# Attention of a gated attention + S4 layer, forward and backward: two interleaved streams of 512-wide tiles with the value products turned round, in held order

## The chip, the cores and the metric

One core of a Trainium2 chip runs the whole program. The metric is device time in microseconds; several runs are taken, beside runs of the kernel before on the same chip. PE is the matmul engine, DVE the vector engine, ACT the engine for exponentials, POOL the general-purpose engine.

## The reference

The program computes the output of `g * attention(x) + (1 - g) * S4(x)` and its gradients. Only attention matters here: sequence 2048, 32 heads of 18 numbers each, bf16.

```python
qkv = (x @ wqkv).reshape(B, S, 3, H, Dh) ...      # H = 32, Dh = 18, S = 2048
scores = einsum("bhqd,bhkd->bhqk", q, k) * Dh ** -0.5
p = softmax(scores)
o = einsum("bhqk,bhkd->bhqd", p, v)
# and by vjp: dV = P^T dO, dP = dO V^T, dS = P * (dP - delta), dQ = dS K, dK = dS^T Q
```

Heads are treated in eight groups of four; each head has 32 rows of the 128 to itself. Per head there are 2048 x 2048 exponentials twice (once with keys on rows, once with queries on rows) and as many products `dS = P * dP` twice. In tiles of 128 x 512 that is 4096 exponentials for ACT and 4096 products for DVE.

## The kernel before

It works in three stages that take turns. Forward (P1): scores, exponential into `PT`, value product. Then dq (P2): dP, product, `dS K`. Then dk/dv (P3): scores, exponential, dP, product, and both value products. The core of P1 and P2 for one block of 512 queries, cut:

```python
for kt in range(NT):                                        # P1
    for u in range(NU):                                     # two halves of 256 columns
        for j in range(4):                                  # row group 32*j holds head j
            mm(pss[j][:, u*256:(u+1)*256], lhsT=KaT_g[r0:r0+DA, kt*P:(kt+1)*P],
               rhs=QaT_g[r0:r0+DA, qs:qs+256], tile_position=(r0, 0))
    for j in range(4):
        nc.scalar.activation(PT[j][:, kt, :], pss[j], ACT.Exp)
    if kt >= 1: pv_step(kt - 1)
def pv_step(kt_):                                           # the value product
    for j_ in range(4):
        for qi_ in range(TPQ):                              # probability tile is the weight,
            mm(oacc[:, j_, qi_, 0:DA], lhsT=PT[j_][:, kt_, qi_*P:(qi_+1)*P],
               rhs=Vtok_g[:, kt_, j_, 0:DA], ...)           # 19 columns move
# ... normalisation, delta, transposes ...
for kt in range(NT):                                        # P2, after all of P1
    ... dP scores into pss; dq_step(kt - 1, ...) ...
    for j in range(4):
        nc.vector.tensor_tensor(dst, pss[j], PT[j][:, kt, :], op=A.mult)
```

The scheduler of the framework may reorder instructions within what the data allow.

Of the kernel before, what the change touches and what calls it, by code (L numbers as in the profile page):

```python
# [9 lines left out]
A = mybir.AluOpType  # L10
# [10 lines left out]
def build(tc, aps, dbg_aps=None, stages=("s1", "attn", "post", "s4", "final")):  # L21
# [39 lines left out]
    with ExitStack() as gctx:  # L61
# [14 lines left out]
        RL = const.tile([P, H, NT], F32, name="RL")  # L76
# [5 lines left out]
        dO_tok = mid1.tile([P, NT, D], BF, name="dO_tok")  # L82
# [6 lines left out]
        Vtok_d = dram.tile([P, NT * H * HP], BF, name="Vtok_d")  # L89
        dqkv_d = dram.tile([P, NT, F], BF, name="dqkv_d")  # L90
# [3 lines left out]
        with ExitStack() as ctx:  # L94
# [127 lines left out]
            for t in range(NT):  # L222
# [5 lines left out]
                for c, (e0, esz) in enumerate(dch):  # L228
                    pt = psB.tile([P, P], BF, tag="tp", name="pt_tp2")
                    nc.tensor.transpose(pt[0:esz, :], d_a_t[:, e0:e0 + esz], ident_bf)  # L230
                    if cnt % 2 == 0:
                        nc.vector.tensor_copy(d_aT[0:esz, c, t * P:(t + 1) * P], pt[0:esz, :])
                    else:
                        nc.scalar.copy(d_aT[0:esz, c, t * P:(t + 1) * P], pt[0:esz, :])
                    cnt += 1
            EW = 48
# [13 lines left out]
            dbg("dO_tok", dO_tok)  # L250
# [5 lines left out]
        if "attn" in stages:  # L256

            DA = DH + 1
            KB = 512
            NQQ = S // KB  # L260
            TPQ = KB // P
            NU = KB // 256
            with ExitStack() as ctx:
                ga = ctx.enter_context(tc.tile_pool(name="ga", bufs=1))
                hp = ctx.enter_context(tc.tile_pool(name="hp", bufs=1))
                hw1 = ctx.enter_context(tc.tile_pool(name="hw1", bufs=1))
                stp = ctx.enter_context(tc.tile_pool(name="stp", bufs=2))
                work = ctx.enter_context(tc.tile_pool(name="awork", bufs=4))
                apsp = ctx.enter_context(tc.tile_pool(name="aps", bufs=1, space=bass.MemoryType.PSUM))

# [3 lines left out]
                cnt = 0  # L274
                for grp in range(NG):
                    QaT_g = ga.tile([P, S], BF, tag="QaT_g", name="QaT_g")
                    KaT_g = ga.tile([P, S], BF, tag="KaT_g", name="KaT_g")
                    VaT_g = ga.tile([P, S], BF, tag="VaT_g", name="VaT_g")
                    nc.sync.dma_start(QaT_g, QaT_d[grp])
                    nc.sync.dma_start(KaT_g, KaT_d[grp])  # L280
                    nc.sync.dma_start(VaT_g, VaT_d[grp])
                    Qtok_g = ga.tile([P, NT, 4, HP], BF, tag="Qtok_g", name="Qtok_g")
                    Ktok_g = ga.tile([P, NT, 4, HP], BF, tag="Ktok_g", name="Ktok_g")
                    Vtok_g = ga.tile([P, NT, 4, HP], BF, tag="Vtok_g", name="Vtok_g")
                    nc.sync.dma_start(Qtok_g, Qtok_v[:, :, 4 * grp:4 * grp + 4, :])
                    nc.sync.dma_start(Ktok_g, Ktok_v[:, :, 4 * grp:4 * grp + 4, :])
                    nc.sync.dma_start(Vtok_g, Vtok_v[:, :, 4 * grp:4 * grp + 4, :])
                    dOa_h = []
                    dOaT_h = []
                    dq_st = []  # L290
                    dk_st = []
                    dv_st = []
                    PT = []
                    for j in range(4):
                        t_ = hw1.tile([P, NT, DA + 1], BF, tag=f"dOa_h{j}", name=f"dOa_h{j}")
                        nc.gpsimd.memset(t_[:, :, DA:DA + 1], 0.0)
                        dOa_h.append(t_)
                        t_ = hw1.tile([P, S], BF, tag=f"dOaT_h{j}", name=f"dOaT_h{j}")
                        dOaT_h.append(t_)
                        dq_st.append(stp.tile([P, NT, DH], BF, tag=f"dq_st{j}", name=f"dq_st{j}"))  # L300
                        dk_st.append(stp.tile([P, NT, DH], BF, tag=f"dk_st{j}", name=f"dk_st{j}"))
                        dv_st.append(stp.tile([P, NT, DH], BF, tag=f"dv_st{j}", name=f"dv_st{j}"))
                        PT.append(hp.tile([P, NT, KB], BF, tag=f"PT{j}", name=f"PT{j}"))
                    for qq in range(NQQ):
                        q0 = qq * KB
                        t0 = qq * TPQ
                        oacc = apsp.tile([P, 4, TPQ, DA + 1], F32, tag="accA", name="oacc")

                        def pv_step(kt_):
                            for j_ in range(4):  # L310
                                for qi_ in range(TPQ):
                                    mm(oacc[:, j_, qi_, 0:DA], lhsT=PT[j_][:, kt_, qi_ * P:(qi_ + 1) * P], rhs=Vtok_g[:, kt_, j_, 0:DA],
                                       start=(kt_ == 0 and j_ == 0 and qi_ == 0), stop=(kt_ == NT - 1 and j_ == 3 and qi_ == TPQ - 1))

                        for kt in range(NT):
                            pss = [apsp.tile([P, KB], F32, tag="blk", bufs=5, name=f"ps_st{j}") for j in range(4)]
                            for u in range(NU):
                                for j in range(4):
                                    r0 = HP * j
                                    qs = q0 + u * 256  # L320
                                    mm(pss[j][:, u * 256:(u + 1) * 256], lhsT=KaT_g[r0:r0 + DA, kt * P:(kt + 1) * P],
                                       rhs=QaT_g[r0:r0 + DA, qs:qs + 256], tile_position=(r0, 0))
                            for j in range(4):
                                nc.scalar.activation(PT[j][:, kt, :], pss[j], ACT.Exp)  # L324
                            if kt >= 1:
                                pv_step(kt - 1)
                        pv_step(NT - 1)
                        for j in range(4):
                            h = 4 * grp + j
                            r0 = HP * j  # L330
                            hc0 = h * DH
                            rl = RL[:, h, t0:t0 + TPQ]
                            nc.vector.reciprocal(rl, oacc[:, j, :, DH])  # L333
                            rlb = rl.unsqueeze(2).to_broadcast([P, TPQ, DH])
                            Oview = O_tok[:, t0:t0 + TPQ, hc0:hc0 + DH]
                            nc.vector.tensor_tensor(Oview, oacc[:, j, :, 0:DH], rlb, op=A.mult)
                            dOa = dOa_h[j]
                            nc.vector.tensor_tensor(dOa[:, t0:t0 + TPQ, 0:DH], dO_tok[:, t0:t0 + TPQ, hc0:hc0 + DH], rlb, op=A.mult)
                            prod = work.tile([P, TPQ, DH], F32, tag="prod", name="prod")
                            nc.vector.tensor_tensor(prod, dOa[:, t0:t0 + TPQ, 0:DH], Oview, op=A.mult)  # L340
                            dl = work.tile([P, TPQ], F32, tag="dl", name="dl")
                            nc.vector.tensor_reduce(dl, prod, axis=AX.X, op=A.add)
                            nc.scalar.mul(dOa[:, t0:t0 + TPQ, DH], dl, -1.0)
                            pT = apsp.tile([P, KB], BF, tag="pT", name="pT")
                            for qi in range(TPQ):
                                nc.tensor.transpose(pT[r0:r0 + DA + 1, qi * P:(qi + 1) * P], dOa[:, t0 + qi, 0:DA + 1], ident_bf,
                                                    tile_position=(0, r0))
                            if j % 2 == 0:
                                nc.scalar.copy(dOaT_h[j][r0:r0 + DA + 1, q0:q0 + KB], pT[r0:r0 + DA + 1, :])  # L349
                            else:  # L350
                                nc.vector.tensor_copy(dOaT_h[j][r0:r0 + DA + 1, q0:q0 + KB], pT[r0:r0 + DA + 1, :])
                        dqacc = apsp.tile([P, 4, TPQ, DA + 1], F32, tag="accB", name="dqacc")

                        def dq_step(kt_, dsts_):
                            for j_ in range(4):
                                for u_ in range(TPQ):
# [4 lines left out]
                        for kt in range(NT):  # L361
# [7 lines left out]
                            if prev_dsts is not None:  # L369
                                dq_step(kt - 1, prev_dsts)  # L370
# [13 lines left out]
                    for kc in range(S // KB):  # L384
# [15 lines left out]
                        for qt in range(NT):  # L400
# [12 lines left out]
                            if prev_ is not None:  # L413
                                dvk_step(qt - 1, prev_[0], prev_[1])
# [690 lines left out]
```

## Time and profile before

| | us |
|---|---|
| median of the timed runs | 8968.7 |
| span of the profiled run | 8949.4 |
| attention in it, first to last | 454 to 5548: 5094 |
| everything else | 3855 |

In attention PE is busy 4982 us, DVE 2716 and ACT 2323. So DVE and ACT together have about as much to do as the stage lasts, but hardly ever at the same time in P1 and P2. The lines that carry this are in the prediction below, with their reading.

### The profile page before, as it was taken

Reading aid. Unit: us, or ns where it says so; the run is one execution under the profiler, and the core shown is the slowest. Engines: PE = TensorE matmul, PEld = TensorE weight load, DVE = VectorE, ACT = ScalarE, POOL = GpSimd, SP = SyncE. Lnnn points to the kernel's source line nnn. Section 1 sums busy time; section 2 is a strip of 40 time slices with the busy share of each in tenths; the row PEclk is TensorE's granted clock in tenths of the full one; section 3 lists DMA queues with packets and bytes.
Section 4 is the critical chain, followed back from the end, with each engine's and each line's share of the span. In section 5 each row is a group of like instructions: output and inputs, shape, how many; then the busy total and the mean of one; then the engine's idle time right before and its main releaser. Section 6 shows DMA issues by size and latency. Waiting matters only on the chain. (4 is left out here: it accounts for less than half of the span.)

```text
span 8949.4 us, 216931 instructions
## 1 busy us (share of the span) xinstructions
PE 6928.2 (77%) x94711; PEld 3868.7 (43%) x94711; DVE 4108.3 (46%) x8636; ACT 3477.3 (39%) x7088; POOL 48.5 (1%) x67
## 2 busy tenths in 40 slices
PE   7799999999999999999999998864443232336773
PEld 5544444444444444444444444753332222236662
DVE  4345455446455455555465554340003777740004
ACT  4344534444444534444534444230001666740001
POOL 0000000000000000000000000000000000000000
PEclk6555555555555555555555555875555555555555
DMA  2101201301301310310211113229996222239997
GB/s 76 72 16 7 9 6 7 13 4 5 14 4 5 13 7 2 14 7 1 13 7 8 7 3 15 90 72 365 384 385 265 83 83 83 93 130 364 372 372 223
DMA packets 502110, 827.64 MB, mean 92 GB/s; under 512 B 295202, under 2 KB 325028, under 8 KB 491428
## 3 DMA queue, kind: packets, MB, share of 16 engines
q1 hardware_dynamic: 501156, 813.76, 32.3%
q8 instruction: 740, 12.12, 0.6%
q14 instruction: 214, 1.75, 0.1%
HBM read 753.09 MB, written 60.56 MB: 91 GB/s over the span
## 5 line engine op out<-in xcount | busy, mean ns | idle before, releaser
L423 DVE TENSOR_TENSOR dsb<-ps_dp,eb 128x512 bf16<-128x512 f32 x2048 | 1325.4, 687 | 1126.4 <-PE ps_dp L30 1009.3
L419 ACT ACTIVATE eb<-ps_s 128x512 bf16<-128x512 f32 x2048 | 1165.9, 596 | 1525.2 <-PE ps_s L30 1503.5
L324 ACT ACTIVATE PT<-ps_st 128x512 bf16<-128x512 f32 x2048 | 1072.7, 611 | 1026.5 <-PE ps_st L30 1021.1
L374 DVE TENSOR_TENSOR dst<-ps_dpt,PT 128x512 bf16<-128x512 f32 x2048 | 1235.2, 697 | 5.5 <-ACT dOaT_h L349 1.2
L30 PE MATMUL ps_dp<-VaT_g,dOaT_h 19*128 19x256 bf16 x4096 | 1014.3, 402 | 0.3
L30 PE MATMUL ps_dpt<-dOaT_h,VaT_g 19*128 19x256 bf16 x4096 | 946.8, 398 | 39.4 <-ACT dOaT_h L349 20.5
L30 PE MATMUL ps_s<-KaT_g,QaT_g 19*128 19x256 bf16 x4096 | 965.3, 402 | 1.0
L30 PE MATMUL ps_st<-QaT_g,KaT_g 19*128 19x256 bf16 x4096 | 927.2, 403 | 15.9 <-DMA KaT_g<-KaT_d 8.1
L30 PEld LDWEIGHTS <-dsb 128*128 128x128 bf16 x8192 | 416.9, 105 | 878.2 <-issue 873.6
L30 PE MATMUL yps<-CXG,HK 128*128 128x16 bf16 x9216 | 553.9, 175 | 231.5 <-issue 154.4
L842 PE MATMUL pt_e<-ident_bf,E1e 128*128 128x128 bf16 x1152 | 186.8, 282 | 689.2 <-ACT E1n L843 350.9
L30 PE MATMUL dkps<-GYREVp,HX 128*128 128x16 bf16 x9216 | 343.0, 175 | 451.8 <-DMA HX<-xpR_d 451.8
L30 PE MATMUL dkacc<-Qtok_g,dsb 128*128 128x18 bf16 x8192 | 647.6, 180 | 0.0
L30 PEld LDWEIGHTS <-HK 128*128 128x128 bf16 x18432 | 528.8, 104 | 274.4 <-issue 170.0
L30 PEld LDWEIGHTS <-dst 128*128 128x128 bf16 x8192 | 338.5, 106 | 602.8 <-issue 602.8
L30 PEld LDWEIGHTS <-PT 128*128 128x128 bf16 x8192 | 329.6, 105 | 595.0 <-issue 588.5
L30 PE MATMUL dxps<-CXG,HK 128*128 128x16 bf16 x9216 | 545.6, 174 | 2.2 <-ACT CXG L914 2.2
L333 DVE RECIPROCAL RL<-oacc 128x4 f32<-128x4 f32 x128 | 22.8, 178 | 1100.1 <-PE oacc L30 1100.1
L30 PEld LDWEIGHTS <-eb 128*128 128x128 bf16 x8192 | 336.1, 105 | 409.9 <-issue 409.9
L30 PEld LDWEIGHTS <-HX 128*128 128x128 bf16 x9216 | 290.5, 105 | 504.8 <-DMA HX<-xpR_d 503.9
L30 PE MATMUL dqacc<-Ktok_g,dst 128*128 128x18 bf16 x8192 | 481.1, 179 | 0.0
L30 PE MATMUL oacc<-Vtok_g,PT 128*128 128x19 bf16 x8192 | 471.4, 182 | 3.4 <-ACT PT L324 0.4
(297 smaller groups left out, 6748.0 us busy)
## 6 DMA issues: line engine op xcount, KB each, us to landing
HX<-xpR_d SPq DMA_DIRECT2D x576, 512.0 KB, 9.6
HK<-Kpad_d SPq DMA_DIRECT2D x576, 512.0 KB, 6.7
abuf<-ath_d SPq DMA_DIRECT2D x36, 1024.0 KB, 4.7
thb<-ath_d SPq DMA_DIRECT2D x36, 1024.0 KB, 4.9
x_tok<-in_A_x_dram SPq DMA_DIRECT2D x3, 2304.0 KB, 9.5
go_t<-in_grad_out_dram SPq DMA_DIRECT2D x48, 144.0 KB, 2.1
dqkv_tok<-dqkv_d SPq DMA_DIRECT2D x1, 6912.0 KB
ga_d<-ga_st SPq DMA_DIRECT2D x16, 288.0 KB, 2.3
```

Source lines behind the costliest of these rows:

```text
L30: return nc.tensor.matmul(out, lhsT=lhsT, rhs=rhs, start=start, stop=stop, **kw)
L324: nc.scalar.activation(PT[j][:, kt, :], pss[j], ACT.Exp)
L333: nc.vector.reciprocal(rl, oacc[:, j, :, DH])
L374: nc.vector.tensor_tensor(dst, pss[j], PT[j][:, kt, :], op=A.mult)
L419: nc.scalar.activation(eb, pss[j], ACT.Exp)
L423: nc.vector.tensor_tensor(dsb, pss2[j], ebs[j], op=A.mult)
L842: nc.tensor.transpose(pt[:, ri, :], E1e[:, ch, ri, :], ident_bf)
```

## The change

Its intent: let ACT and DVE work at once, so that neither waits out the other's stage, and use PE's array by placing heads side by side, in row groups for the scores and column groups for the value products. Core of the diff:

```diff
+ctx.enter_context(tc.manual_schedule(engines={PE, Activation, DVE, Pool}))   # order as written
-for j_ in range(4): for qi_ in range(TPQ):
-    mm(oacc[:, j_, qi_, 0:DA], lhsT=PT[j_][:, kt_, qi_*P:(qi_+1)*P], rhs=Vtok_g[:, kt_, j_, 0:DA])
+mm(acc[HP*j:HP*(j+1), :], lhsT=st[:, i, j, :], rhs=mv, ..., tile_position=(0, HP*j))  # token tile is
+                                                     # the weight (32 wide), 512 columns move
+blocks: (P1(g,b), P2(g,b-1)), (P3S(g-1,b), P3D(g-1,b)), ...    # exponential and product stream
+for (a_, d_) in blocks:
+    for i in range(NT):
+        for jj in ((0, 1), (2, 3)):                            # one step: two heads
+            act_s.append((a_, i, jj))
+            dve_s.append((d_, i, jj))
+act_s.append((None, 0, ()))
+dve_s.insert(0, (None, 0, ()))                                 # product stream one step behind
+for n in range(len(act_s) + LAG):
+    score matmuls of step n (2 + 2 heads); value products of step n - LAG; exponentials and products of n
+    # transposes back and gradient copies come in small pieces, one every third step
```

(Cuts: loads, normalisation and the pieces. All after attention is the same code.)

## The prediction

> **What bounds the kernel now.** I read the page first: busy time of the engines, then the 40 slices, then the costliest groups.
>
> ```profile
> PE 6928.2 (77%) x94711; PEld 3868.7 (43%) x94711; DVE 4108.3 (46%) x8636; ACT 3477.3 (39%) x7088; POOL 48.5 (1%) x67
> ...
> PE   7799999999999999999999998864443232336773
> ...
> PEclk6555555555555555555555555875555555555555
> ...
> L423 DVE TENSOR_TENSOR dsb<-ps_dp,eb 128x512 bf16<-128x512 f32 x2048 | 1325.4, 687 | 1126.4 <-PE ps_dp L30 1009.3
> L419 ACT ACTIVATE eb<-ps_s 128x512 bf16<-128x512 f32 x2048 | 1165.9, 596 | 1525.2 <-PE ps_s L30 1503.5
> L324 ACT ACTIVATE PT<-ps_st 128x512 bf16<-128x512 f32 x2048 | 1072.7, 611 | 1026.5 <-PE ps_st L30 1021.1
> L374 DVE TENSOR_TENSOR dst<-ps_dpt,PT 128x512 bf16<-128x512 f32 x2048 | 1235.2, 697 | 5.5 <-ACT dOaT_h L349 1.2
> ```
>
> The page's chain of waits covers only the last 58 us (it starts at 8891), so it says nothing of attention; I used the times of first and last instruction of the attention tiles instead. Attention runs from 453.8 (first ps_st) to about 5548 (last gradient copies): 5094 us of 8949.4. The other 3855 us are code that the diff leaves alone. Then I asked for the busy time in single stages: a forward pass of one block of 512 queries (all four heads of a group), the dq pass of the next, and a dk/dv pass, and the whole of attention.
>
> ```profile
> 454.00:494.00 40.00, 36.92 (x394) 15.88 (x387) 2.93 (x19) 33.52 (x68) 0.00 (x0) 0.50 0.22 44
> ...
> 576.00:618.00 42.00, 41.44 (x412) 18.48 (x411) 38.77 (x66) 3.61 (x7) 0.00 (x0) 0.50 0.01 2
> 777.00:854.00 77.00, 77.00 (x768) 33.65 (x767) 42.15 (x69) 37.10 (x67) 0.00 (x0) 0.50 0.33 12
> ...
> 454.00:5548.00 5094.00, 4982.28 (x49681) 2211.47 (x49674) 2715.51 (x5000) 2322.68 (x4486) 6.15 (x29) 0.50 0.15 7
> ```
>
> Columns: stretch, length, busy PE, weight loads, DVE, ACT, POOL, then the granted clock. The three stages take turns: forward keeps ACT busy (33.5 of 40) while DVE has nothing; the dq pass keeps DVE busy (38.8 of 42) while ACT has nothing; dk/dv has PE full (77 of 77) and both others half idle. Sixteen tiles of four heads per pass give 2.5, 2.6 and 4.8 us. The clock is 0.50 in all of them, however full PE is. How full PE is in truth shows in order of time:
>
> ```profile
> 520.39 0.29 PEld L30 LDWEIGHTS <-dst 128*128 128x128 bf16 x8 [0.41 <-issue]
> ...
> 520.70 0.19 PEld L30 LDWEIGHTS <-VaT_g 19*128 19x128 bf16 x4
> ...
> 521.30 0.19 PEld L30 LDWEIGHTS <-dst 128*128 128x128 bf16 x4 [0.41 <-issue]
> ...
> 790.29 0.12 PEld L30 LDWEIGHTS <-dOaT_h 19*128 19x128 bf16 x2
> ...
> 790.82 0.18 PEld L30 LDWEIGHTS <-dsb 128*128 128x128 bf16 x4 [0.41 <-issue]
> ...
> 791.03 0.12 PEld L30 LDWEIGHTS <-QaT_g 19*128 19x128 bf16 x2
> ```
>
> From one head's two 256-column score matmuls to the next weight load is 0.53 us (790.29 to 790.82); four of them, two heads in different row groups, take 0.60 (520.70 to 521.30). So heads in different row groups do overlap. The small matmuls that follow cost 0.31 for eight and 0.21 for four, so about 26 ns each and 0.10 fixed. Two streams of 256 columns at half of 2.4 GHz are 0.427, so 0.10 to 0.17 of each score block is also a change-over.
>
> **What the skill says.** "TensorE: Matmul & The Clock Gate", section on the back-to-back issue gap: N columns take N/1.2 ns at the half clock and N/2.4 at the full one. The trace agrees at half clock as far as the 0.53 shows. Its Part 3 on packing: tiles in different row groups run together (3.07 times for four) and so do tiles in different column groups (2.38 for three). For rows the trace agrees (0.60 against 0.53); column tiles don't occur before, so no run shows them yet. "TensorEngine Tiling (Array Packing)", Key Properties: a change of tiling mode drains the array; that fits the fixed 0.10 us. Part 1 of the clock page: the clock goes to full after about 3.4 us of activity. The trace limits this: 0.50 through a PE that counts as 100% busy in dk/dv, and 1.00 only in later stages with dense 128-row matmuls (30 per us of 128x48 turned it up within four microseconds at 5597; 15 per us of 128x54 at 50 to 100 us left it at 0.50).
>
> **The change, part by part.** Kept: 4096 exponentials and 4096 products of 512 columns. Removed: 32768 matmuls of 18 or 19 columns, each with a full weight load, and the halving of score matmuls. Added: the value, dq, dk and dv products turned round: weights are the 32-wide token tile, the moving operand is the 512-wide tile, output goes to 32 PSUM rows per head in a column group of its own; 8192 of these, beside 8192 score matmuls of 512 columns. The output is transposed back in pieces. Moved: every step now pairs two heads of an exponential stream with two heads of a product stream, so ACT and DVE work at once. The built order of PE confirms: four score matmuls, then four value matmuls of two steps earlier.
>
> Limits of one step: ACT 2 x 0.597 = 1.19 us; DVE 2 x 0.69 = 1.38. PE at half clock: score part, two row groups, each two tiles of 427 ns one after the other, plus 0.13 change-over, about 0.99; value part, two column groups, again 2 x 0.427, plus 0.10, about 0.96. Sum 1.95 us. So PE bounds, not DVE, as long as the clock is at half: only two of four groups are in use at a time, because the two streams of a step have the same two heads.
> There are 65 blocks of 32 steps: 63 full ones, 63 x 32 x 1.95 = 3931. The first has only the forward stream (32 x 1.2 = 38), one near the end only dq (32 x 1.4 = 45). 28 empty steps of the first group, where transposed output is waited for: 20. Pieces on PE: 32 times four fp32 transposes (estimate 1.9 us, four passes each), 32 times four bf16 ones (0.65), 48 times eight (1.06): 61 + 21 + 51 = 133. Sum 4167 against 5094. Extra work of ACT (accumulator copies, about 130 us) and DVE lies beside it; POOL gets two small products per block, covered by the pieces' delay of several steps. With 3855 for the rest and 19 us between the profile's span and the timed median: 8041.
>
> **Rivals.**
> 1. The clock rises. PE streams 1.71 of 1.95 us, 88%, against some 65% in dk/dv before. If the monitor counts streaming of any tile, this may be enough; if it weighs the part of the array in use (a quarter per tile, so 44% of the array's columns and rows here), it isn't. At full clock a step needs about 1.1 us on PE and DVE bounds at 1.38: 2016 x 1.40 = 2822, plus 38, 45, 20 and about 100 for DVE's own extras and pieces, 3025 in all; total 6900. For: Part 1 of the page. Against: 0.50 at every moment of attention before, with PE called full.
> 2. The clock swings: full clock makes PE wait for DVE, its activity falls to 60%, it is throttled again. 7300 to 7600.
> 3. Column tiles don't overlap. Then the value part is 4 x 0.427 + 0.10 = 1.81 and the step 2.8: attention 5900, total 9800, slower. Only the skill speaks against it.
> 4. Emission order stalls: scores have three PSUM buffers per stream, and the second score matmul of a step waits for the first exponential of the step before. At 1.95 us that exponential is long done, so it costs nothing while PE bounds; pieces that borrow a score buffer (112 of them) could each cost up to a microsecond, 100 us.
>
> **Range and chances.** I give the half clock 0.6 (7850 to 8250), full clock 0.25 (near 6900), a swing 0.1, no overlap or something unforeseen 0.05. The median of that lies at the lower edge of the first: 7900. Four times in five within 6850 to 8250. Faster by over 2% in all but the last: 0.94; within 2% 0.02; slower 0.04.
>
> **What would show it.** Attention from about 455 to 4620 us with PE near 100% busy, clock 0.50, ACT and DVE each around 60 to 70% and waiting for PE: main line right. Clock near 1.0 in those slices, DVE near 95% and PE waiting for DVE: rival 1. Value matmuls starting one after another at 0.43 us: rival 3. The 1.95 is wrong if a change-over is not near 0.1 us, and the sum if the PE waits for ACT or DVE between score matmuls. The slices after attention must be the same as before.

## The result, and the profile after

The changed kernel takes 6800.0 us (median of 4 runs, 6798.8 to 6805.5); before, on the same chip, 8968.7. The ratio is 0.7583, 95% interval 0.7573 to 0.7594. Ratios are the mean time of one kernel's fast runs over that of the other's of the same rounds, so not quite the ratio of the medians. The predicted 7900 was too slow, and 6800 lies just outside the range of 6850 to 8250.

First the page of the changed kernel: engines, the slices with the clock, and the first groups.

```profile
PE 4762.3 (70%) x62071; PEld 2257.4 (33%) x62071; DVE 4011.0 (59%) x7837; ACT 3479.8 (51%) x6912; POOL 101.5 (1%) x133
...
DVE  4328999989898989899943500002678767200005
ACT  3347878878787878786833300001866685300001
...
PEclk6555555555555555555578655555555555555555
...
L398 DVE TENSOR_TENSOR ds<-ps_P3D,eb 128x512 bf16<-128x512 f32 x2048 | 1293.3, 686 | 128.3 <-PE ps_P3D L30 83.7
L390 ACT ACTIVATE PT<-ps_P 128x512 bf16<-128x512 f32 x2048 | 1107.8, 596 | 211.9 <-PE ps_P L30 113.4
```

DVE is now at 0.8 to 0.9 and more in nearly every slice of attention. Its idle time before the dk/dv products fell from 1126 us (group L423 of before) to 128, and ACT's before the forward exponentials from 1027 (L324) to 212. Each product still takes 686 ns, each exponential 596. The clock row still says half. Attention as one stretch:

```profile
454.00:3408.00 2954.00, 2814.82 (x17004) 596.72 (x17005) 2614.68 (x4192) 2321.17 (x4301) 53.73 (x97) 0.50 0.06 13
```

The last gradient copies leave at 3416 us, so attention takes 2962 us instead of 5094, that is 2132 less; the whole span is 2151 less. So practically all of the gain comes from attention, as predicted. DVE is busy 2615 of the 2954 us in this window, 89%. PE's 2815 (95%) is no measure of its load, as two steps in order of time show:

```profile
1000.02 0.61 PE L30 MATMUL accA<-eb,dOa 128*32 128x512 bf16 x2
...
1000.02 0.61 PE L30 MATMUL accB<-ds,Qtok_g 128*32 128x512 bf16 x2
1000.56 0.10 PEld L30 LDWEIGHTS <-QaT_g 19*128 19x128 bf16 x2 [0.43 <-issue]
1000.56 0.61 PE L30 MATMUL ps_P3S<-KaT_g,QaT_g 19*128 19x512 bf16 x2
...
1000.57 0.78 PE L30 MATMUL ps_P3D<-VaT_g,dOaT_g 19*128 19x512 bf16 x2
...
1001.27 0.11 PEld L30 LDWEIGHTS <-dOa 128*32 128x32 bf16 x2 [0.60 <-issue]
```

All four value matmuls start at 1000.02 and the first three score matmuls 0.54 us later: 0.54 us for four tiles of 512 columns. The prediction expected two and two, 0.96 and 0.99 us. The fourth score matmul begins 0.20 us after the third (the pair spans 0.78 instead of 0.61 from first start to last end), as it waits for DVE (so the built order says: its PSUM buffer, a bank of the memory that matmuls write to, is the one that an earlier product reads). Between 900 and 2900 us the four scores of a step are spread like this in 95% of the steps, by 0.22 us in the median. Where they are not, the four take 0.54 us. So PE has slack, and DVE sets the pace.

The same view for DVE (one row for four products):

```profile
1040.70 2.52 DVE L398 TENSOR_TENSOR ds<-ps_P,PT 128x512 bf16<-128x512 f32 x4
```

Back to back a product costs 0.63 us, not the 0.69 of one alone. A block of P1 with P2 has 64 of them, 40.3 us; such blocks take 42.5 us (from the first exponential of one block to that of the next; median of 28). Blocks of P3, in which the transposes and copies fall, take 46.5 us (median of 27).

### The profile page after: what moved, and what is told of

Its sections match the earlier page's. It is cut to its first block, busy times and chain, and to the rows that moved or that the text cites.

```text
span 6798.7 us, 147781 instructions
## 1 busy us (share of the span) xinstructions
PE 4762.3 (70%) x62071; PEld 2257.4 (33%) x62071; DVE 4011.0 (59%) x7837; ACT 3479.8 (51%) x6912; POOL 101.5 (1%) x133
## 3 DMA queue, kind: packets, MB, share of 16 engines
q14 instruction: 184, 1.51, 0.1%
## 5 line engine op out<-in xcount | busy, mean ns | idle before, releaser
L398 DVE TENSOR_TENSOR ds<-ps_P3D,eb 128x512 bf16<-128x512 f32 x2048 | 1293.3, 686 | 128.3 <-PE ps_P3D L30 83.7
L398 DVE TENSOR_TENSOR ds<-ps_P,PT 128x512 bf16<-128x512 f32 x2048 | 1288.3, 686 | 101.5 <-PE ps_P L30 97.0
L394 ACT ACTIVATE eb<-ps_P3S 128x512 bf16<-128x512 f32 x2048 | 1109.2, 596 | 259.8 <-PE ps_P3D L30 179.1
L390 ACT ACTIVATE PT<-ps_P 128x512 bf16<-128x512 f32 x2048 | 1107.8, 596 | 211.9 <-PE ps_P L30 113.4
L30 PE MATMUL ps_P3D<-VaT_g,dOaT_g 19*128 19x512 bf16 x2048 | 790.8, 593 | 16.4 <-DVE ds L398 15.8
L30 PE MATMUL ps_P<-dOaT_g,VaT_g 19*128 19x512 bf16 x2048 | 757.9, 592 | 0.0
L30 PE MATMUL ps_P<-QaT_g,KaT_g 19*128 19x512 bf16 x2048 | 676.0, 597 | 72.1 <-DMA KaT_g<-KaT_d 37.7
L30 PE MATMUL ps_P3S<-KaT_g,QaT_g 19*128 19x512 bf16 x2048 | 671.0, 597 | 31.0 <-ACT eb L394 28.5
L30 PE MATMUL dkps<-GYREVp,HX 128*128 128x16 bf16 x9216 | 343.2, 175 | 456.4 <-DMA HX<-xpR_d 456.4
L30 PE MATMUL dxps<-CXG,HK 128*128 128x16 bf16 x9216 | 545.4, 174 | 145.7 <-issue 143.3
L30 PE MATMUL accA<-PT,Vtok_g 128*32 128x512 bf16 x2048 | 625.0, 608 | 6.0 <-DMA Vtok_g<-Vtok_d 5.8
L30 PE MATMUL accB<-ds,Qtok_g 128*32 128x512 bf16 x2048 | 626.7, 608 | 0.0
L30 PE MATMUL accA<-eb,dOa 128*32 128x512 bf16 x2048 | 626.7, 608 | 0.0
L30 PE MATMUL accB<-ds,Ktok_g 128*32 128x512 bf16 x2048 | 625.2, 608 | 0.0
L30 PEld LDWEIGHTS <-HK 128*128 128x128 bf16 x18432 | 528.3, 104 | 264.8 <-DMA HK<-Kpad_d 144.2
L30 PE MATMUL yps<-CXG,HK 128*128 128x16 bf16 x9216 | 549.9, 175 | 79.5 <-DMA HK<-Kpad_d 77.5
L30 PEld LDWEIGHTS <-HX 128*128 128x128 bf16 x9216 | 290.7, 105 | 509.5 <-DMA HX<-xpR_d 508.5
```

Of the source, the lines that this page charges most:

```text
L30: return nc.tensor.matmul(out, lhsT=lhsT, rhs=rhs, start=start, stop=stop, **kw)
L390: nc.scalar.activation(out, ps, ACT.Exp)
L394: nc.scalar.activation(out, ps, ACT.Exp)
L398: nc.vector.tensor_tensor(out, ps, e, op=A.mult)
```

## The experiments

Block lengths below are read in this way. The runs were made in four sittings, in which the median of the kernel before lay between 8941 and 8984 us; so differences between two variants are worked out from their ratios, times 8968.7. Two theories had to be told apart: that four different heads stand side by side in a step, because the product stream is one step behind (mine, after the result), or that PE is simply faster than the prediction's sum, or DVE or order matter in some other way.

**1. The same heads in both streams.** The product stream is put two steps behind, not one; two steps are one round of heads (0, 1), (2, 3).

```diff
-act_s.append((None, 0, ()))
-dve_s.insert(0, (None, 0, ()))
+for _ in range(2):
+    act_s.append((None, 0, ()))
+    dve_s.insert(0, (None, 0, ()))
```

> The changed kernel with the product stream two steps behind the exponential stream instead of one, so that both streams of a step hold the same two heads, as the prediction had wrongly assumed. Theory (four heads side by side is what makes PE cheap): score part and value part of a step take two tiles one after the other per row or column group, step 1.95 us by the prediction's own sum, attention about 4170 us, whole 8000 us (7850 to 8200), PE full, DVE idle about a third. Rival (PE streams faster than the sum thinks, whatever the groups): within 2% of the changed kernel, 6800 us.

8077.1 us (ratio 0.8989, 0.8976 to 0.9003), correct. PE in order of time:

```profile
1000.80 0.61 PE L30 MATMUL ps_P<-QaT_g,KaT_g 19*128 19x512 bf16 x2
...
1001.20 0.63 PE L30 MATMUL ps_P<-dOaT_g,VaT_g 19*128 19x512 bf16 x2
...
1001.77 0.61 PE L30 MATMUL accA<-PT,Vtok_g 128*32 128x512 bf16 x2
...
1002.17 0.63 PE L30 MATMUL accB<-ds,Ktok_g 128*32 128x512 bf16 x2
...
1002.74 0.61 PE L30 MATMUL ps_P<-QaT_g,KaT_g 19*128 19x512 bf16 x2
```

The second pair now starts 0.40 us after the first, in the scores and in the value products, and the step is 1.94 us. The prediction's sum of 1.95 us a step and 8041 us in all describes this kernel, within half a per cent. By the ratios it lies 1261 us above the changed kernel ((0.8989 - 0.7583) x 8968.7): the worth of one inserted empty step.

**2. A control: three steps behind.** Different heads again, but a longer lag (same edit with 3).

> A control for the run with two steps of shift: three steps, so that the two streams of a step hold different heads again, but the product stream lags by more. Theory (which heads share a step decides): back at the changed kernel's time, 6760 to 6860 us. Rival (the longer lag was what cost 1280 us): 8000 us or more.

7341.4 us (0.8210, 0.8198 to 0.8223): between the two. The blocks say why. Those of P3 were back at 46.6 us in the median (65.5 with two steps), but those of P1/P2 took 59.7. The waits of 2000 us in the middle name it:

```profile
ACT PT L390 <- DVE ds L398: 413.3, 239, 1.8
```

The longer lag keeps probability tiles longer than the 18 buffers allow. So I gave it 19.

```diff
-ptp = ctx.enter_context(tc.tile_pool(name="ptp", bufs=18))
+ptp = ctx.enter_context(tc.tile_pool(name="ptp", bufs=19))
```

> The control again, with 19 probability tiles instead of 18: with three steps of shift and 18 tiles ACT waited 413 us per 2000 for the products to free them, and the forward blocks took 59.7 us, while the dk/dv blocks, which use no such tiles, were back at 46 to 47 against 65.5 with two steps. Theory (which heads share a step decides, the lag by itself costs nothing once there is a tile for it): dk/dv blocks about 46.5, forward blocks 42.5 to 44, whole 6780 to 6880 us. Rival (the lag costs in itself): 7200 us or more.

6815.1 us (0.7624, 0.7611 to 0.7637); P1/P2 blocks 42.65, P3 blocks 46.6 in the median. The lag by itself costs nothing; which heads share a step decides.

The run with 18 tiles holds a trap. Its clock row reads differently from all others:

```profile
PEclk9999999999999999999976875555555555555555
```

Yet its four value tiles take the same 0.55 us (value matmuls at 1100.65, the first score matmuls at 1101.20). The packed trace explains the row: this run's clock records begin only at 3745 us, and the view shows full clock where there is no record. (The 1.00 of the kernel before up to 44 us is such a gap too; the prediction's "only in later stages" passes over it.) So the spacing of matmuls has to confirm the row. The Trainium skill, "TensorE: Matmul & The Clock Gate", Part 1, warns in its trace caveats that the recorded events can be unreliable; this run, with no record for its first 3745 us, agrees.

That the spacing does tell the clock is shown by four other runs (experiments 3, 6, 8 and the second form of 7), whose records have full clock inside attention for 6.8 to 23.9 us at a time. In the second form of 7, where only dq was left to do and a group is two tiles, a group took 0.54 us at half clock (3010.05 to 3010.59) and 0.32 soon after; four tiles in experiment 6 took 0.33 (2346.28 to 2346.61):

```profile
3015.40:3036.00 20.60, 19.66 (x136) 6.00 (x136) 17.89 (x28) 5.77 (x12) 0.20 (x1) 1.00 0.02 4
...
3015.32 0.39 PE L30 MATMUL ps_P<-dOaT_g,VaT_g 19*128 19x512 bf16 x2
3015.64 0.39 PE L30 MATMUL accB<-ds,Ktok_g 128*32 128x512 bf16 x2
3015.96 0.39 PE L30 MATMUL ps_P<-dOaT_g,VaT_g 19*128 19x512 bf16 x2
```

Each of these rises came within a microsecond after rounds of eight gradient transposes; that they caused it isn't shown, and in the changed kernel the same transposes brought no such record before the very last ones, at 3410 us.

**3. One stream at a time.** P2 and P1 blocks one after the other, all else as changed.

```diff
-if p1 or p2: blocks.append((p1, p2))
+if p2: blocks.append((None, p2))
+if p1: blocks.append((p1, None))
```

> The forward pass and the dq pass run one after the other again, all else as in the changed kernel. Theory (most of the gain is that ACT and DVE work at once): forward block 32 x 1.17, dq block 32 x 1.3, dk/dv block 32 x 1.3; 32 times 121 us = 3870, with fill 3900 to 4000 us of attention, whole 7700 to 7900 us. Rival (the gain is in the larger matmuls): within 3% of 6800 us.

7860.3 us (0.8748, 0.8734 to 0.8763), as computed. Its waits between 900 and 2900 us show the taking of turns again: `DVE ds L398 <- ACT eb L394: 643.0` and `ACT PT L390 <- PE ps_P L30: 582.1`, both with single waits of 35 to 41 us, a whole block. Working at once in P1 and P2 is worth 1045 us ((0.8748 - 0.7583) x 8968.7).

**4. The value products as before, in the interleaved order.** The tile is the weight again, four matmuls of 32 columns per tile; no transposing back.

```diff
-mm(acc[HP*j:HP*(j+1), :], lhsT=st[:, i, j, :], rhs=mv, ..., tile_position=(0, HP*j))
+for qi in range(TPQ):
+    o0 = (j*TPQ + qi) * HP
+    mm(acc[:, o0:o0+HP], lhsT=mv[:, qi*P:(qi+1)*P], rhs=st[:, i, j, :], ...)
```

> The two interleaved streams kept, but the value products as before: the 128-wide tile is the weight, 32 columns of tokens move, four matmuls and full weight loads per tile, no transposes after. Right result. Theory: the trace of before has such matmuls start every 26 ns, so 16 x 0.026 + 0.1 = 0.52 us a step against 0.54 for the turned form; the step stays DVE-bound and the whole is within 2% of 6800 us, perhaps a little faster as transposes fall away. Rival (turning the value products is where the gain is): 16 full weight loads at 0.105 us make the step over 2 us and the whole over 8300 us.

6721.0 us (0.7482, 0.7471 to 0.7493), correct, and 1.3% faster than the changed kernel by the ratios. A step of it:

```profile
1010.01 0.29 PEld L30 LDWEIGHTS <-PT 128*128 128x128 bf16 x8 [0.44 <-issue]
...
1010.22 0.29 PEld L30 LDWEIGHTS <-ds 128*128 128x128 bf16 x8
...
1010.55 0.61 PE L30 MATMUL ps_P<-QaT_g,KaT_g 19*128 19x512 bf16 x2
```

Sixteen weight loads with their small matmuls take from 1010.01 to 1010.55: 0.54 us, as much as four turned matmuls side by side. So turning the value products round, half of the diff's idea, gains nothing here; going back saves 91 us by the ratios, and with it the transposes fall away.

**5. Same heads, old value products.** The edits of 1 and 4 together, to part the row groups from the column groups.

> Two steps of shift (same heads in both streams), with the value products of before, which use the whole array one after the other. Theory (score tiles that share row groups cost 0.43 us more a step, value tiles that share column groups another 0.43, and full-array value products cost 0.54 whatever the heads): step 0.99 + 0.54 = 1.53 us, blocks about 49 us and more with pieces, whole 7050 to 7250 us, that is about half way between 6721 and 8077. Rival (the loss of the two-step run lies in waits, not in the groups): as the two-step run, 8000 us, or as the one without it, 6720.

7191.6 us (0.8044, 0.8032 to 0.8056), blocks of 51 to 52 us. A step takes PE 1.5 us:

```profile
1100.02 0.61 PE L30 MATMUL ps_P<-QaT_g,KaT_g 19*128 19x512 bf16 x2
1100.42 0.64 PE L30 MATMUL ps_P<-dOaT_g,VaT_g 19*128 19x512 bf16 x2
1100.98 0.39 PE L30 MATMUL accA<-Vtok_g,PT 128*128 128x32 bf16 x8
...
1101.52 0.61 PE L30 MATMUL ps_P<-QaT_g,KaT_g 19*128 19x512 bf16 x2
```

Between 4 and this lie 504 us by the ratios, put down to scores that share row groups; between this and run 1 lie 848, put down to value products that share column groups. The first is smaller because DVE's step of 1.33 us hides part of PE's rise from 1.08 to 1.51; from 1.51 to 1.94 nothing hides, and 2048 steps of 0.43 are 880. The sizes are not quite clean: run 1 alone has the transposes back, and here ACT waits for probability tiles (172 us in 2000), as in experiment 2. P3 blocks use no such tiles. The last ones, with no forward pass between them and few pieces, took 63.9 us in run 1, 50.4 here and 43.2 in experiment 4, that is 0.42 and 0.23 us a step, in line with the above.

**6. No held order.** The line with `manual_schedule` is taken out.

> The changed kernel without holding the engines to emission order; the scheduler may move instructions. Theory (the gain needs the four tiles of a step to stand side by side in PE's queue): the scheduler breaks up some fours, the whole is slower, 6950 to 7800 us. Rival (order is of no account once the streams are written interleaved): within 2% of 6800 us.

9835.6 us (1.0998, 1.0980 to 1.1016): slower than before the change, and far beyond what either theory expected. PE in order of time:

```profile
2001.57 0.63 PE L30 MATMUL ps_P<-dOaT_g,VaT_g 19*128 19x512 bf16 x1
...
2002.13 0.61 PE L30 MATMUL accB<-ds,Ktok_g 128*32 128x512 bf16 x1
...
2002.67 0.60 PE L30 MATMUL ps_P<-QaT_g,KaT_g 19*128 19x512 bf16 x1
...
2003.20 0.61 PE L30 MATMUL accA<-PT,Vtok_g 128*32 128x512 bf16 x1
...
2003.74 0.60 PE L30 MATMUL ps_P<-dOaT_g,VaT_g 19*128 19x512 bf16 x1
```

Here the scheduler lines up one score matmul and one value matmul in turn. Each of these 512-column matmuls then pays 0.54 us alone, though four together pay the same. Between 900 and 2900 us, 86% of the groups of one kind are of one or two matmuls, and 3% of four; in the changed kernel practically all are of four. The trace counts PE as busy all the time, and only 685 steps' worth of exponentials come out of 2000 us (1408 in the changed kernel). The held order is therefore no refinement of this change but a condition of it.

**7. Is it DVE that bounds?** Half of the products are left out (wrong result). In the first form the value product of every second head reads the exponential tile instead.

```diff
+elif j % 2 == 1:
+    out = T["PT"][(b, i)][:, j, :] if kind == "P2" else e3.pop((g, b, i, j))
```

> Wrong result on purpose: every second head's product is left out, its value matmul reads the exponential tile instead; all matmuls and exponentials stay. Theory (DVE bounds at 1.29 to 1.36 us a step): the bound passes to ACT (2 x 0.55) and PE (1.09), step 1.10 to 1.25 us, attention 2350 to 2650 us, whole 6200 to 6500 us. Rival (PE bounds, it is 96% busy in the page): unchanged within 2%, 6800 us.

6854.0 us (0.7627, 0.7616 to 0.7638): no faster, as the rival said. But this edit holds probability tiles longer, a new wait that the changed kernel doesn't have (`ACT PT L390 <- PE accB L30: 258.0` in 2000 us). The second form reads the neighbour head's product tile, which holds nothing longer.

> Wrong result on purpose: as the first run with half of the products, but every second head's value matmul now reads the neighbour head's product tile, so that no probability tile is held longer than in the changed kernel (in the first run ACT waited 258 us per 2000 for such tiles and the forward blocks became longer, 48.4 against 42.5 us, though the dk/dv blocks became shorter, 41.5 against 45.2). Theory (DVE bounds the forward blocks at 64 x 0.645 = 41.3; with half of it ACT bounds at about 1.17 a step as in the very first block): forward block 37.5 to 40, dk/dv block 40 to 44, attention 2550 to 2750, whole 6400 to 6600 us. Rival (the order of PE and its buffers bound, whatever DVE has to do): within 2% of 6800 us.

6596.9 us (0.7375, 0.7364 to 0.7386). P1/P2 blocks 40.4 us, a little above what was expected, plain P3 blocks 41.5 (45.2 in the changed kernel). So DVE does set the pace, but halving its work buys 3%: a next limit, at about 1.26 us a step, lies close behind. Which one isn't shown; in this profile ACT is busy 1716 of 2000 us and waits often and briefly for scores (`ACT PT L391 <- PE ps_P L30: 68.4, 325, 0.3`). (This run passed the comparison with the reference although half of its products were replaced. That comparison doesn't resolve this error, so passing it is not proof that the dq and dk of a variant are right.)

**8. Taking work off DVE.** One product in twelve goes by ACT (copy to bf16) and POOL (multiplication), value products three steps late.

```diff
+if pc[0] % 12 == 0:
+    nc.scalar.copy(cp, ps); nc.gpsimd.tensor_tensor(out, cp, e, op=A.mult)
```

> One product in twelve is taken off DVE: ACT copies the score tile to bf16, POOL multiplies; value products come three steps later instead of two. Right result. Theory (DVE bounds, ACT has room): DVE needs 64 x 11/12 x 0.645 = 37.9 us a block, ACT 34.8 + 5.3 x 0.55 = 37.7 plus its waits of about 0.1 a step; block 40 to 42, whole 6620 to 6760 us. Rival (ACT and DVE are already in balance through PE's order): 6800 us or more.

7020.6 us (0.7852, 0.7840 to 0.7863), slower than the changed kernel. Two things were changed at once; the later value products alone were not run. PE in order of time:

```profile
1100.22 0.60 PE L30 MATMUL ps_P3D<-VaT_g,dOaT_g 19*128 19x512 bf16 x1
1101.18 0.58 PE L30 MATMUL ps_P3D<-VaT_g,dOaT_g 19*128 19x512 bf16 x1 [0.36 <-ACT cp L402]
1101.69 0.61 PE L30 MATMUL accA<-PT,Vtok_g 128*32 128x512 bf16 x2
```

The copy stands behind two exponentials in ACT's order, the score buffer comes free late, and PE, in order itself, holds everything behind it: value products start 1.49 us after the scores, not 0.54. The busy sums said there was room on ACT; in this stretch the order of three engines said there was not. How much of the 241 us (by the ratios) this wait makes isn't shown. With the old value products it is the same:

> Value products of before in the interleaved order, with one product in twelve on ACT and POOL: the two things that should each help. Right result. Theory: 6721 us less 60 to 180 us, 6540 to 6680 us. Rival (no room on ACT): 6700 us or more.

6815.7 us (0.7622, 0.7610 to 0.7633) against 6721 without, again with both edits.

**9. A better version.** Experiment 4 with less of DVE's extra work: the output's multiplication and the gradient copies on POOL, the reduction some steps later.

> The value products of before in the interleaved order (6721 us), with DVE's extra work between blocks made less: the multiplication of the output and the gradient copies go to POOL, the reduction comes some steps later so that DVE doesn't wait 1.07 us per block for POOL. Theory (DVE bounds): 32 x (0.46 + 1.07) = 49 us less, 6640 to 6700 us. Rival (those gaps lie beside other waits): 6700 to 6730 us.

6682.8 us (0.7472, 0.7460 to 0.7485), correct, the fastest of all. By its ratio it is 1.5% below the changed kernel; against experiment 4 the ratios' intervals overlap, so that step alone isn't settled by them, but in the profiles the last scores of attention start at 3287 instead of 3326 us, 38 us earlier, near the 49 expected. The three edits were not tried singly.

## Why the prediction was wrong

- **Where the gain lies** was right: attention only, 2132 of 2151 us, the rest nearly unchanged.
- **What the change does to ACT and DVE** was right: run side by side in P1 and P2, worth 1045 us (experiment 3). The other large part is P3, where PE was full before: its 32 blocks fell from 77 to 46.5 us, 976 us in all. No run takes this alone; experiments 1 and 4 show that it needs four different heads side by side, but not the turned products.
- **The step that failed** is this: "only two of four groups are in use at a time, because the two streams of a step have the same two heads." The code inserts one empty step ahead of the product stream. With pairs (0, 1) and (2, 3) in turn, that puts heads 2 and 3 of one stream beside heads 0 and 1 of the other. PE's step was then not 1.95 us but 0.54 + 0.54, and the bound not PE but DVE, at 1.33 us a step. I had read the built order of PE, but in it matmuls carry the names of tensors, not the row groups; the heads of a step had to be worked out from the two lists.
- **The sum itself** was right for the kernel that it described: 8041 us against 8077 measured in experiment 1. Halved groups, 0.43 us a stream at half clock and 0.10 to 0.13 for a change-over were all sound: 0.40 and 0.57 us were measured where 0.43 and 0.53 to 0.56 were expected. That the total is so close is partly luck: attention took 4240 us against 4167, and the terms for the rest of the program made up half of that. One small term was wrong: four fp32 transposes start 0.21 us apart in the changed kernel, so about 0.9 us and not 1.9.
- **Rival 1** named almost the time that came, 6900, with DVE as the bound, but from a clock that rises. The clock didn't rise: it is recorded as 0.50 from 48 to 3410 us, when only the last transposes of attention are left, and four tiles take 0.54 us, not the 0.33 seen where it did rise (experiment 2). The right bound followed from the wrong cause; that the number was near is luck. Its average of 1.40 us a step, and 3025 us of attention against 2962, were good because DVE sets it in either case.
- **Rival 3**, column tiles that don't overlap, is refuted by 0.54 us for four. Rival 2, a swing, is not in the changed kernel's attention; the short rises of four other runs (7 to 24 us) are the nearest to it. **Rival 4**, pieces that cost up to a microsecond each, is real: P1/P2 blocks with four gradient pieces take 45.9 to 46.3 us instead of 42.5, some 0.9 us a piece; in experiment 4, where the pieces borrow no score buffer and transpose nothing, 43.0 to 43.3 instead of 42.2. Of the 4 us by which P3 blocks are longer, pieces explain only a part: the last ones, with no forward pass between them, still take 43.9.

## What to carry to other kernels

Before estimating PE for tiled arrays, write down for each group of neighbouring matmuls which row and column groups they occupy; a shift by one step was worth 1261 us. If such neighbours matter, the order has to be held, since here the scheduler's reordering undid more than the whole gain. And before moving work to an engine that looks idle in the sums, ask where it will stand in that engine's order and whose buffer it holds until then.

## What the Trainium skill lacked or had wrong

- "TensorEngine Tiling (Array Packing)", Key Properties: it says that a change of tiling mode drains the array, but gives no time for it. Here four row tiles (19 rows, 512 columns), followed by four column tiles (32 wide, 512 columns) and so on in turn, cost 0.54 us each group where nothing waits, change-over included, and a single one of either kind in such a turn also costs 0.54 (experiment 6). The price of alternating kinds one by one is not on the page.
- "TensorE: Matmul & The Clock Gate", Part 1: full clock after about 3.4 us of sustained activity. In experiment 1 PE streamed two tiles of four without a pause of note (1768 of 1800 us busy, two streams of 0.40 us in each 0.97) for thousands of microseconds, and the spacing stayed at half clock. The page says that transposes don't count as busy in the same way (Part 4), but not whether streaming through half of the row or column groups counts.
- The same page, LDWEIGHTS: it gives 128 columns at 1.2 GHz, and a measured factor of about two for fast loading. In experiment 4 sixteen loads of 128 columns, each with a 32-column matmul, took 0.54 us, 34 ns a pair with the change-over and 27 ns from one to the next, though each load is recorded with 0.10 us. Small matmuls with full loads were as cheap as four packed large ones; the advice to swap the operands and tile the columns ("TensorEngine Tiling (Array Packing)", Performance Considerations) has no such comparison.
- Its caveat on recorded clock events doesn't say that records can be missing from the start: one run has none before 3745 us, and the view then shows full clock at an unchanged spacing of matmuls (0.55 us for four tiles). Nor does it name the spacing as a check, which told 0.54 from 0.33 us (experiment 2).
